# A DeltaNet and Fourier-mix kernel: the block inversion's products as 32x32 blocks, one PE tile each

## Chip, cores and metric

The kernel runs on one core of a Trainium2 chip. The metric is the device time of one execution in microseconds; the profile's span runs from the first to the last instruction of one profiled execution. TensorE (PE in the profile, its weight loads PEld) multiplies matrices, VectorE (DVE), ScalarE (ACT) and GpSimd (POOL) do the elementwise work, SyncE (SP) starts transfers.

## What is computed

Two steps, in float32. First a recurrence per batch and head (4 batches, 8 heads, 768 tokens of 48 values): a 48x48 state is read with the query and then corrected with the key and the value.

```python
k_n = k / (norm(k) + 1e-06)
for t in range(S):
    y[:, :, t] = einsum('bhd,bhde->bhe', q[:, :, t], state)
    v_old = einsum('bhde,bhd->bhe', state, kt)
    state = state + bt * einsum('bhd,bhe->bhde', kt, vt - v_old)
```

The eight heads' outputs lie side by side in a row of 384 values, x. Then, per batch: `mixed = real(fft(fft(x, axis=1), axis=2))`, `u = x + mixed`, a layer norm of u, a two-layer MLP with a ReLU and 1536 hidden values, and u added to its output.

## The kernel before

The tokens of a batch are cut into 6 chunks of 128 (`C`), so there are 24 steps. Three pieces of work belong to a step; each is a Python generator that emits instructions up to its next `yield`.

`pre(n)` (line 232) makes what a chunk needs that doesn't depend on the state. It normalises the keys and scales them with beta, transposes keys and queries on TensorE into `K1T` and `KQT` (lines 256 to 262; two heads of a pair lie in the row halves 0 to 47 and 64 to 111), and forms the Gram products `pg` (lines 269 to 284): for each kind a (keys with keys, keys with queries) and each row half e, four products of 48 rows, one per pair of heads. From them come `Abd` (masked to the diagonal 32x32 blocks), `AT` and `LQ`. Then it inverts the four diagonal 32x32 blocks of I + A of each head, doubling the inverted block from 1 to 32 in five levels (lines 297 to 327). In a level, `px` gets the identity (line 301: a bf16 product with 128x128 weights and 256 columns) and, added to it, A times the inverse so far, T, one product per head; VectorE masks it to `Y` (line 305); `pn` gets the new transposed inverse (half 0, line 315) and, in the three middle levels, the new inverse itself (half 1, line 312); ScalarE copies it to `Tn`. T and its transpose TT are views of `Tn`.

The blocks are kept in two forms. A compact tile has the four 32x32 blocks of a head one below the other on the 128 partitions, 32 columns in all. A wide one, made by `widen` (line 289), has them on the diagonal of 128x128, with zeros elsewhere: it multiplies the compact tile by a mask, five heads on VectorE and three on GpSimd. A product has a wide tile, 128x128, as its weights and a compact one, 32 columns, as what is streamed through them. `Abd` is wide from the start; `Yx` and `TTx` are the widened Y and TT.

`seq(n)` (line 330) is the chunk's step of the recurrence: it solves the triangular system with the inverted blocks, four blocks of 32 tokens in turn (`pu`, 32x32 weights; `pa`, 32 columns of weights), each with a ScalarE copy or a VectorE subtraction between, and then updates the state (`pS`, 128x64 weights, even heads to partitions 0 to 63, odd ones to 64 to 127) and computes the output (`py`).

`post(b)` (line 383) is the second part of a batch: the Fourier products `pf` and `pb`, the layer norm, the MLP's `ph` and `po`.

The loop (lines 477 to 493) advances `seq(n)`, `pre(n+1)` and a share of 13 units (`UNITS`) of a side generator in turn. That is `weights()` in batch 0, which turns the float64 weights into float32 on VectorE and GpSimd, and `post(b-1)` later; the last `post` stands alone at the end. The tile framework places what is emitted in each engine's queue, moving instructions against each other where their data allows it, and adds the semaphore waits.[...] PSUM tiles of `pre` share three buffers (`ps_pre`), those of `seq` two, those of `post` three.

Of the kernel before, what the change touches and what calls it, by code (L numbers as in the profile page):

```python
# [13 lines left out]
ALU = mybir.AluOpType  # L14
ACT = mybir.ActivationFunctionType

C = 128          # tokens of a chunk
W = 32           # width of the diagonal blocks that are inverted explicitly
LEVELS = (1, 2, 4, 8, 16)


def _consts(S, DM):
    """Constants of the shapes: identity, masks and Fourier tables."""
    p = np.arange(128)
    c = np.arange(W)
    r = p % W
    ident = np.eye(128)
    su = (p[None, :] > p[:, None]).astype(np.float64)
    bd = su * (p[None, :] // W == p[:, None] // W)
    grp = (p[:, None] // W == np.arange(128 // W)[None, :]).astype(np.float64)  # L30
    eye_c = (r[:, None] == c[None, :]).astype(np.float64)
    lev = []
    for n in LEVELS:
        off = ((r[:, None] // n) % 2 == 1) & (c[None, :] // n == r[:, None] // n - 1)
        lev.append(eye_c - off)
    pack = np.concatenate([ident, su, bd, grp, eye_c] + lev, axis=1)

    half = S // 2
    s = np.arange(half)

    def seq_table(ks):
        ang = 2.0 * np.pi * (np.outer(s, ks) % S) / S
        t = np.concatenate([np.cos(ang), np.sin(ang)], axis=1)
        return t.reshape(half // 128, 128, -1).transpose(1, 0, 2)

    d = np.arange(DM)
    ang = 2.0 * np.pi * (np.outer(d, d) % DM) / DM
    dt = np.stack([np.cos(ang), -np.sin(ang)])
    dt = dt.reshape(2, DM // 128, 128, DM).transpose(2, 0, 1, 3)

    def f32(a):
        return np.ascontiguousarray(a, dtype=np.float32)

    return dict(pack=f32(pack), even=f32(seq_table(np.arange(0, half + 1, 2))),
                odd=f32(seq_table(np.arange(1, half, 2))), dtab=f32(dt))
# [3 lines left out]
def kernel(  # L59
# [22 lines left out]
    NE = HALF // 2 + 1  # L82
    NO = HALF // 2
    GT = 2
    HV = (5 * H + 7) // 8

    cn = {n: nc.inline_tensor(a, name="k_" + n) for n, a in _consts(S, DM).items()}

# [18 lines left out]
        nc.tensor.matmul(o, lhsT=src, rhs=ident[0:src.shape[0], 0:src.shape[0]],  # L107
                         is_transpose=True, start=start, stop=True, skip_group_check=True)

# [1 line left out]
    NKQ = 2  # L111
    kqs = []
    for i in range(NKQ):
# [43 lines left out]
    nc.scalar.dma_start(out=odt, in_=cn["odd"].ap())  # L157
    nc.scalar.dma_start(out=dtab, in_=cn["dtab"].ap())

    # 0 and 1 are exact in bf16: these only put the identity into an accumulation  # L160
    ident_b = const.tile([128, 128], BF16, name="ident_b")
    nc.vector.tensor_copy(ident_b, ident)
    eye_b = const.tile([128, H, W], BF16, name="eye_b")
# [3 lines left out]
    half_n = const.tile([128, GT], F32, name="half_n")  # L167
    nc.gpsimd.memset(half_n, -0.5)

    # beta with the tokens of a chunk on the partitions  # L170
    psb = ps_pre([128, NC, NBH], "psb")
    for c in range(NC):
        tr(psb[:, c, :], bt[:, c * C:(c + 1) * C], c == 0)
# [1 line left out]
    nc.vector.tensor_copy(bcol.rearrange("p c b h -> p c (b h)"), psb)  # L175

    def weights():
        """The weights come as float64, which no engine computes with: the bits are taken
        apart and each value is rounded to the nearest float32, the widest type there is.
        Float32 weights are loaded as they are."""  # L180
        if moe_w_ch1.dtype == F32:
            nc.sync.dma_start(out=w1, in_=moe_w_ch1.rearrange("(c p) f -> p c f", p=128))
            nc.sync.dma_start(out=w2, in_=moe_w_ch2.rearrange("(c p) m -> p c m", p=128))
# [14 lines left out]
        for i, (_, dst) in enumerate(pieces):  # L198
            w64 = nxt
            if i + 1 < len(pieces):  # L200
                nxt = staged(i + 1)
            lo, hi = w64[:, :, 0], w64[:, :, 1]
            tmp = wk.tile([128, 3, DFF], I32, tag="F", name="wtmp")
            man, exp, low = tmp[:, 0], tmp[:, 1], tmp[:, 2]
            # 1.m from the high word's 20 bits of the mantissa; the low word's added, rounding
            nc.vector.tensor_scalar(man, hi, 3, 0x007FFFF8, op0=ALU.logical_shift_left,
                                    op1=ALU.bitwise_and)
            nc.vector.tensor_scalar(man, man, 0x3F800000, None, op0=ALU.bitwise_or)
            yield
            nc.vector.tensor_scalar(low, lo, 8, None, op0=ALU.logical_shift_right)  # L210
            nc.vector.scalar_tensor_tensor(man.bitcast(F32), low, 2.0 ** -44, man.bitcast(F32),
                                           op0=ALU.mult, op1=ALU.add)
            yield
            # the signed power of two, 0 below float32's range
            nc.vector.tensor_scalar(exp, hi, 20, 0x7FF, op0=ALU.logical_shift_right,
                                    op1=ALU.bitwise_and)
            nc.vector.tensor_scalar(exp, exp, 896, 0, op0=ALU.subtract, op1=ALU.max)
            yield
            nc.vector.tensor_scalar(exp, exp, 255, None, op0=ALU.min)
            nc.vector.tensor_scalar(exp, exp, 23, None, op0=ALU.logical_shift_left)  # L220
            yield
            nc.vector.tensor_scalar(low, hi, 31, 31, op0=ALU.logical_shift_right,
                                    op1=ALU.logical_shift_left)
            nc.vector.tensor_tensor(exp, exp, low, op=ALU.bitwise_or)
            nc.gpsimd.tensor_tensor(dst.rearrange("p c f -> p (c f)"), man.bitcast(F32),
                                    exp.bitcast(F32), op=ALU.mult)
            yield
# [2 lines left out]
    xs = {}  # L230

    def pre(n):
        """What a chunk needs that does not depend on the state."""
        b, c = steps[n]
        kq = kqs[n % NKQ]
        K4, V4 = loaded.pop(n)
# [24 lines left out]
            nc.scalar.activation(dst, pt, ACT.Copy)  # L261
            yield

        # AT[s, h, t] = beta_t k_t.k_s;  LQ[s, h, t] = q_t.k_s for s < t
        AT = wk.tile([128, H, 128], F32, tag="AT", bufs=2, name="AT")
        LQ = wk.tile([128, H, 128], F32, tag="LQ", bufs=2, name="LQ")
        Abd = wk.tile([128, H, 128], F32, tag="Abd", name="Abd")
        hv = "p (j e) t -> p e j t"
        for a in range(2):
            for e in range(2):  # L270
                pg = ps_pre([128, NP, 128], "pg")
                pr = slice(64 * e, 64 * e + D)
                for j in range(NP):
                    mm(pg[:, j, :], K1T[pr, j, :], KQT[pr, a, j, :], j == 0)
                if a == 0:
                    nc.vector.tensor_tensor(Abd.rearrange(hv, e=2)[:, e], pg,
                                            m_bd[:, None, :].broadcast_to([128, NP, 128]),
# [2 lines left out]
                else:  # L280
                    nc.vector.tensor_tensor(LQ.rearrange(hv, e=2)[:, e], pg,
                                            m_su[:, None, :].broadcast_to([128, NP, 128]),
                                            op=ALU.mult)
                yield

        # T = (I + A)^-1 of the diagonal blocks, doubling the block:
        # T2n = Tn Y with Y = I - (A between the halves) Tn. Compact tiles hold
        # only the diagonal blocks; wide ones are block diagonal.
        def widen(src, tag):
            t = wk.tile([128, H, NG, W], F32, tag=tag, name=tag)  # L290
            for eng, hs in ((nc.vector, slice(0, HV)), (nc.gpsimd, slice(HV, H))):
                shape = [128, hs.stop - hs.start, NG, W]
                eng.tensor_tensor(t[:, hs], src[:, hs, None, :].broadcast_to(shape),  # L293
                                  m_grp[:, None, :, None].broadcast_to(shape), op=ALU.mult)
            return t.rearrange("p h g w -> p h (g w)")

        T = TT = TTx = None
        for i in range(len(LEVELS)):
            last = i == len(LEVELS) - 1
            px = ps_pre([128, H, W], "px")  # L300
            mm(px, ident_b, eye_b, True, False)
            for h in range(H):
                mm(px[:, h, :], Abd[:, h, :], eye_c if T is None else T[:, h, :], False, h == H - 1)
            Y = wk.tile([128, H, W], F32, tag="Y", bufs=2, name="Y")
            nc.vector.tensor_tensor(Y, px, m_lev[i][:, None, :].broadcast_to([128, H, W]),  # L305
                                    op=ALU.mult)
            Yx = widen(Y, "Yx")
            yield
            pn = ps_pre([128, 2, H, W], "pn")
            if i > 0 and not last:  # L310
                for h in range(H):
                    mm(pn[:, 1, h, :], TTx[:, h, :], Y[:, h, :], h == 0)
                yield
            for h in range(H):
                mm(pn[:, 0, h, :], Yx[:, h, :], eye_c if TT is None else TT[:, h, :],
                   h == 0 and (i == 0 or last))
            Tn = wk.tile([128, 2, H, W], F32, tag="Tn", bufs=3, name="Tn")
            if i == 0 or last:
                nc.scalar.activation(Tn[:, 0], pn[:, 0], ACT.Copy)
# [2 lines left out]
                nc.scalar.activation(Tn, pn, ACT.Copy)  # L322
                T = Tn[:, 1]
            TT = Tn[:, 0]
            if not last:
                TTx = widen(TT, "TTx")
            yield
        ready[n] = (kq, KQT, AT, LQ, TT, Vb)

    def seq(n):  # L330
        """The chunk's step of the recurrence."""
        b, c = steps[n]
        kq, KQT, AT, LQ, TT, Vb = ready.pop(n)
        st = states[b % 2]
# [46 lines left out]
    out_v = out.rearrange("b (t p) m -> b t p m", p=128)  # L381

    def post(b):
        """Fourier mixing, layer norm and channel MLP of one batch."""
        x = xs.pop(b)
        # cos and sin at s + S/2 are those at s, with the sign (-1)^k
        pm = wk.tile([128, 2, TH, DM], F32, tag="big", bufs=2, name="pm")
        nc.vector.tensor_tensor(pm[:, 0], x[:, 0:TH], x[:, TH:2 * TH], op=ALU.add)
        nc.gpsimd.tensor_tensor(pm[:, 1], x[:, 0:TH], x[:, TH:2 * TH], op=ALU.subtract)
        # F[d, 0, :, k] = sum_s x cos, F[d, 1, :, k] = sum_s x sin  # L390
        F = wk.tile([128, 2, KD, S], F32, tag="F", name="F")
        for dt in range(KD):
            for par, tab, n, hi in ((0, evt, NE, HALF + 1), (1, odt, NO, HALF)):
# [65 lines left out]
                nc.vector.tensor_tensor(x[:, T, :], x[:, T, :], po, op=ALU.add)  # L459
                nc.sync.dma_start(out=out_v[b, T], in_=x[:, T, :])  # L460

    # ---- the chunks of a batch in turn; beside each step, the next chunk's
    # preparation and a share of the previous batch's second part (at first, of the
    # weights' conversion) ----
    UNITS = (2 * KD + 2 * NC + (NC // GT) * (1 + KF + 3 * GT)) // NC + 1

    def advance(gen, n=1):
# [58 lines left out]
```

## Time and profile before

| | before |
|---|---|
| time, median of 2 runs | 1848.38 us (1840.3 and 1856.46) |
| span of the profiled execution | 1847.0 us |
| instructions | 26294 |
| TensorE matmul and weight load busy | 96% and 81% of the span |
| VectorE, ScalarE, GpSimd busy | 31%, 14%, 25% |
| DMA | 32.76 MB, mean 18 GB/s |

A group line of the profile names line, engine and operation, then the tile written and the tiles read (buffer numbers left out), shapes, and the count; behind the bar come the busy time in us and the mean of one in ns, then the time that the engine sat idle before these instructions and what ended it. All matmuls carry line 104, that of the helper `mm`, and transposes line 107, so they are told apart by their tiles. A float32 product appears as two weight loads and two matmuls. Records of neighbouring matmuls overlap, since each is shown from its start to the modelled end of its last result; the distance from start to start is the pace. Slices (part 2) show the busy share in tenths, PEclk the granted share of TensorE's clock.

### The profile page before, as it was taken

What the parts mean: (1) busy time and instruction counts of PE and PEld (TensorE: products, weight loads), DVE (VectorE), ACT (ScalarE), POOL (GpSimd) and SP (SyncE); (2) the same over time, 40 slices, a digit from 0 to 9 for tenths busy, and PEclk for the clock granted to TensorE, in tenths of its full rate; (3) what the DMA queues carried; (4) which work ended last, traced back from release to release, by engine and by line L of the source; (5) the groups of instructions that cost most, each with busy time, mean ns of one, the idle gap of its engine ahead of it and who ended that gap; (6) DMA issues with size and microseconds to landing.
All of it is one profiled execution on the core that took longest, in us unless ns stands there. A gap on an engine that the chain in (4) does not pass through costs nothing. (4 is left out here: it accounts for less than half of the span.)

```text
span 1847.0 us, 26294 instructions
## 1 busy us (share of the span) xinstructions
PE 1773.4 (96%) x11830; PEld 1503.7 (81%) x11830; DVE 578.4 (31%) x919; ACT 253.0 (14%) x505; POOL 453.0 (25%) x356
## 2 busy tenths in 40 slices
PE   4898889989999999999999999999999999999999
PEld 4888889889887897888877897888787888888676
DVE  4534741212123431333232433333323423222211
ACT  1011010101111101101112111111120111111110
POOL 4413422222132230232132231232223212212000
PEclk9999999999997976998798999998999999999999
DMA  7101100000000000000000000000000000000000
GB/s 209 39 9 43 43 5 9 14 5 13 5 1 14 10 9 13 14 14 18 9 9 14 10 9 18 14 22 10 9 10 13 10 10 6 5 6 5 5 9 18
DMA packets 81088, 32.76 MB, mean 18 GB/s; under 512 B 75440, under 2 KB 78512, under 8 KB 80464
## 3 DMA queue, kind: packets, MB, share of 16 engines
q1 hardware_dynamic: 80352, 28.32, 6.1%
q10 hardware_dynamic: 624, 2.76, 0.4%
q8 instruction: 93, 1.52, 0.4%
q14 instruction: 19, 0.16, 0.0%
HBM read 26.35 MB, written 4.72 MB: 17 GB/s over the span
## 5 line engine op out<-in xcount | busy, mean ns | idle before, releaser
L104 PEld LDWEIGHTS pn<-Tn,Yx 128*128 128x128 f32 x1536 | 229.5, 233 | 27.3 <-issue 13.9
L293 POOL TENSOR_TENSOR Yx<-Y,pack 128x384 f32<-128x384 f32 x120 | 166.4, 1386 | 306.4 <-DVE Y L305 286.3
L104 PE MATMUL pn<-Tn,Yx 128*128 128x32 f32 x1536 | 225.7, 307 | 13.8 <-DVE Yx L293 13.8
L104 PE MATMUL ph<-unT,w 128*128 128x256 f32 x864 | 235.5, 414 | 2.0 <-ACT unT L438 2.0
L293 POOL TENSOR_TENSOR TTx<-Tn,pack 128x384 f32<-128x384 f32 x96 | 127.6, 1330 | 372.9 <-ACT Tn L322 314.9
L104 PE MATMUL po<-w,hT 128*128 128x384 f32 x576 | 208.9, 504 | 0.0
L104 PEld LDWEIGHTS px<-Tn,Abd 128*128 128x128 f32 x1152 | 172.8, 235 | 27.2 <-ACT Tn L322 18.4
L104 PEld LDWEIGHTS pn<-Y,TTx 128*128 128x128 f32 x1152 | 168.8, 231 | 22.2 <-DVE Y L305 19.1
L293 DVE TENSOR_TENSOR TTx<-Tn,pack 128x640 f32<-128x640 f32 x96 | 84.6, 881 | 326.4 <-ACT Tn L322 278.3
L104 PE MATMUL px<-Tn,Abd 128*128 128x32 f32 x1152 | 173.5, 311 | 13.3 <-ACT Tn L322 13.3
L104 PEld LDWEIGHTS ph<-unT,w 128*128 128x128 f32 x864 | 164.2, 203 | 25.6 <-ACT unT L438 2.7
L104 PE MATMUL pn<-Y,TTx 128*128 128x32 f32 x1152 | 170.7, 308 | 10.3 <-DVE Y L305 10.3
L104 PEld LDWEIGHTS po<-w,hT 128*128 128x128 f32 x576 | 105.7, 194 | 59.9 <-issue 3.0
L104 PE MATMUL pg<-KQT,K1T 48*128 48x128 f32 x768 | 137.3, 348 | 2.8 <-ACT KQT L261 2.8
L104 PEld LDWEIGHTS pg<-KQT,K1T 48*128 48x128 f32 x768 | 111.6, 236 | 17.2 <-ACT KQT L261 4.4
L293 DVE TENSOR_TENSOR Yx<-Y,pack 128x640 f32<-128x640 f32 x120 | 119.7, 997 | 8.2
L305 DVE TENSOR_TENSOR Y<-px,pack 128x256 f32<-128x256 f32 x120 | 50.7, 423 | 216.6 <-PE px L104 216.5
L104 PE MATMUL pb<-dtab,F 128*128 128x384 f32 x288 | 118.2, 551 | 0.0
L322 ACT ACTIVATE Tn<-pn 128x512 f32<-128x512 f32 x72 | 43.0, 597 | 527.1 <-PE pn L104 527.1
L104 PEld LDWEIGHTS pu<-R,Tn 32*32 32x32 f32 x1280 | 72.4, 123 | 29.6 <-issue 13.2
L248 POOL TENSOR_TENSOR kq<-kq,bcol 128x384 f32<-128x384 f32 x24 | 21.8, 910 | 279.4 <-DVE kq L246 250.3
L352 DVE TENSOR_TENSOR R<-R,pa 32x384 f32<-32x384 f32 x60 | 33.2, 553 | 182.4 <-PE pa L104 182.3
(88 smaller groups left out, 1833.8 us busy)
## 6 DMA issues: line engine op xcount, KB each, us to landing
w<-in_moe_w_ch_dram SPq DMA_DIRECT2D x6, 1536.0 KB, 6.5
K<-in_k_dram SPq DMA_DIRECT2D x24, 192.0 KB, 2.6
V<-in_v_dram SPq DMA_DIRECT2D x24, 192.0 KB, 2.6
kq<-in_q_dram SPq DMA_DIRECT2D x24, 192.0 KB, 2.8
out_dram<-x SPq DMA_DIRECT2D x24, 192.0 KB, 1.9
dtab<-k_dtab ACTq DMA_DIRECT2D x1, 1152.0 KB, 8.3
evt<-k_even ACTq DMA_DIRECT2D x1, 579.0 KB, 5.7
odt<-k_odd ACTq DMA_DIRECT2D x1, 576.0 KB, 6.9
```

The lines of the kernel that those rows point to most:

```text
L104: nc.tensor.matmul(o, lhsT=lhsT, rhs=rhs, start=start, stop=stop, skip_group_check=True)
L248: nc.gpsimd.tensor_tensor(kq[:, 1, :, 0:D], kq[:, 0, :, 0:D], bc[:, :, None].broadcast_to([128, H, D]), op=ALU.mult)
L293: eng.tensor_tensor(t[:, hs], src[:, hs, None, :].broadcast_to(shape), m_grp[:, None, :, None].broadcast_to(shape), op=ALU.mult)
L305: nc.vector.tensor_tensor(Y, px, m_lev[i][:, None, :].broadcast_to([128, H, W]), op=ALU.mult)
L322: nc.scalar.activation(Tn, pn, ACT.Copy)
L352: nc.vector.tensor_tensor(R[rw], R[rw], pa[rw], op=ALU.subtract)
```

## The change

The four diagonal blocks of a head no longer go through one product with 128x128 weights, but through four with 32x32 weights. Block g lies on partitions 32g to 32g+31 of the weights, of the streamed tile and of the output, which is the PE tile of row group g and column group g. So the compact tiles serve as weights too, and the wide ones, `widen` and its mask, fall away. A px or pn block of 8 products becomes one of 32, in the order of heads and, inside a head, of tiles. `pn`'s first write in each 32-partition group starts the accumulation there. In the middle levels half 1 comes before half 0, as before. What is meant: products of different tiles may run beside each other in the array, weights are a quarter as wide, and VectorE and GpSimd lose the widening.

The Gram products now take both PSUM tiles of a kind at once and alternate between the row halves, so that neighbours use different rows of the array; the two masks and copies follow after all eight.

The yields move with it: two instead of four in the Gram part, 18 instead of 13 in the levels. Comments are dropped as well, which moves later lines by one or more.

```diff
@@ pre(n), Gram products
         for a in range(2):
+            pgs = [ps_pre([128, NP, 128], f"pg{e}") for e in range(2)]
+            for j in range(NP):
+                for e in range(2):
+                    pr = slice(64 * e, 64 * e + D)
+                    mm(pgs[e][:, j, :], K1T[pr, j, :], KQT[pr, a, j, :], j == 0)
             for e in range(2):
-                pg = ps_pre([128, NP, 128], "pg")
-                pr = slice(64 * e, 64 * e + D)
-                for j in range(NP):
-                    mm(pg[:, j, :], K1T[pr, j, :], KQT[pr, a, j, :], j == 0)
+                pg = pgs[e]
...
-                yield
+            yield
@@ pre(n), inversion
-        def widen(src, tag):
...
-        T = TT = TTx = None
+        def blocks(o, lhsT, rhs):
+            for h in range(H):
+                for g in range(NG):
+                    rw = slice(W * g, W * g + W)
+                    mm(o[rw, h, :], lhsT(h, g, rw), rhs(h, g, rw), False)
+
+        T = TT = None
...
-            for h in range(H):
-                mm(px[:, h, :], Abd[:, h, :], eye_c if T is None else T[:, h, :], False, h == H - 1)
+            blocks(px, lambda h, g, rw: Abd[rw, h, rw],
+                   (lambda h, g, rw: eye_c[rw]) if T is None else
+                   (lambda h, g, rw: T[rw, h, :]))
...
-            Yx = widen(Y, "Yx")
             yield
             pn = ps_pre([128, 2, H, W], "pn")
-            if i > 0 and not last:
+            first = [True] * NG
+            for a in ((1, 0) if i > 0 and not last else (0,)):
                 for h in range(H):
-                    mm(pn[:, 1, h, :], TTx[:, h, :], Y[:, h, :], h == 0)
+                    for g in range(NG):
+                        rw = slice(W * g, W * g + W)
+                        left, right = (TT, Y) if a else (Y, TT)
+                        r = eye_c[rw] if right is None else right[rw, h, :]
+                        mm(pn[rw, a, h, :], left[rw, h, :], r, first[g])
+                        first[g] = False
                 yield
-            for h in range(H):
-                mm(pn[:, 0, h, :], Yx[:, h, :], eye_c if TT is None else TT[:, h, :],
-                   h == 0 and (i == 0 or last))
...
-            if not last:
-                TTx = widen(TT, "TTx")
             yield
```

## The prediction

> **What bounds the kernel now.** I read the page's busy times first, then its slices, the groups, and the timeline for the pace of single blocks.
>
> ```profile
> PE 1773.4 (96%) x11830; PEld 1503.7 (81%) x11830; DVE 578.4 (31%) x919; ACT 253.0 (14%) x505; POOL 453.0 (25%) x356
> ...
> PEclk9999999999997976998798999998999999999999
> ```
>
> TensorE is busy 96% of the span; no other engine passes a third. The groups tell with what:
>
> ```profile
> L104 PEld LDWEIGHTS pn<-Tn,Yx 128*128 128x128 f32 x1536 | 229.5, 233 | 27.3 <-issue 13.9
> L293 POOL TENSOR_TENSOR Yx<-Y,pack 128x384 f32<-128x384 f32 x120 | 166.4, 1386 | 306.4 <-DVE Y L305 286.3
> L104 PE MATMUL pn<-Tn,Yx 128*128 128x32 f32 x1536 | 225.7, 307 | 13.8 <-DVE Yx L293 13.8
> L104 PE MATMUL px<-Tn,Abd 128*128 128x32 f32 x1152 | 173.5, 311 | 13.3 <-ACT Tn L322 13.3
> L104 PE MATMUL pn<-Y,TTx 128*128 128x32 f32 x1152 | 170.7, 308 | 10.3 <-DVE Y L305 10.3
> ...
> L293 DVE TENSOR_TENSOR Yx<-Y,pack 128x640 f32<-128x640 f32 x120 | 119.7, 997 | 8.2
> ```
>
> With the px and pn groups of the first level these are 742 us of TensorE time: a product loads 128x128 weights to stream 32 columns. Each fp32 product is two passes (1536 records for 768 products), each a weight load and a matmul. A chunk has 13 blocks of eight products, 5 of px and 8 of pn: 208 passes. Means of overlapping records overstate, so I take paces from the timeline (start, length, count):
>
> ```profile
> 468.96 3.62 PE L104 MATMUL px<-Tn,Abd 128*128 128x32 f32 x16 [0.75 <-ACT Tn L322]
> 473.10 3.62 PE L104 MATMUL pn<-Y,TTx 128*128 128x32 f32 x16 [0.52 <-DVE Y L305]
> ```
> ```profile
> 736.18 2.83 PE L104 MATMUL po<-w,hT 128*128 128x384 f32 x8
> 738.84 1.87 PE L104 MATMUL pn<-pack,Yx 128*128 128x32 f32 x16
> 740.54 2.83 PE L104 MATMUL po<-w,hT 128*128 128x384 f32 x8
> ```
> ```profile
> 861.09 0.67 PE L104 MATMUL pS<-U,kq 128*64 128x48 f32 x16
> ```
> ```profile
> 773.91 0.86 PE L104 MATMUL pu<-R,Tn 32*32 32x48 f32 x16
> 774.71 0.76 PE L107 MATMUL pt<-pack,kq 128*128 128x128 f32 x5
> ```
> ```profile
> 776.80 0.38 PE L104 MATMUL ph<-unT,w 128*128 128x256 f32 x1
> 777.11 0.27 PE L104 MATMUL pu<-R,Tn 32*32 32x48 f32 x2
> ```
>
> A block of 16 passes takes 3.4 us from start to start at 470 us and 1.7 to 1.8 at 739 us; single records there are 213 and 112 ns apart. The first is a TensorE at half its clock, although PEclk shows 9 there: the trace's clock records begin at 529 us. So the time has three parts. To 558 us, the first preparation and batch 0's six chunks run at half clock, with little between the blocks. By the first transpose of each preparation in the timeline (86.8, 557.7, 1623.1 us) these six take 78.5 us each. From 558 to about 1690 us, 17 preparations, 66.6 us each, have the previous batch's post work beside them, mostly at full clock. After that comes the end of the post work, which the change doesn't touch. All three are set by TensorE's in-order queue.
>
> **What the Trainium skill says.** "TensorEngine Tiling (Array Packing)", Key Properties: tiles work independently, and a change of tiling mode drains TensorE. The trace agrees: the step from the last ph pass to the first 32x32 pu pass is 309 ns, where ph passes are 216 apart (93 more), and the step back from pu to 128x128 is 131 ns. "TensorE: Matmul & The Clock Gate", section LDWEIGHTS, makes a load's time proportional to its columns: 112 ns per pass with 128 columns; in pS, where two tiles of 64 columns alternate, each tile repeats every 58. Its Part 3 has matmuls of different tiles overlap, with starts 4 ns apart; in pS they start 7 to 8 ns apart, in pairs, and 16 passes start within 0.45 us, so two column tiles of one bank do overlap. Its Part 1 has the clock either at half or full by recent activity; the 213 and 112 ns agree.
>
> **The change, part by part.**
> (1) px and pn: each product becomes four 32x32 products on four tiles, so a block has 64 passes in place of 16. What one tile needs: pu streams 48 columns in 43 ns (40 plus 2.5), so 32 columns take 29; a 32-column load, by 112 and 58, also about 29. Four tiles side by side thus need 29/4 = 7.3 ns per pass, the lower bound: 0.47 us a block. The upper bound is the densest stream the trace has, pS: 58 ns for two passes, 29 each, 1.86 us a block. In pS, bursts of single instructions start 7 to 8 ns apart, and a pair of load and matmul 7 ns after the last, so I expect the queue to hand out a pass every 7 to 15 ns, and take 10: 0.64 us at full clock. At half clock a tile needs 58 ns, four tiles 14.6 per pass; I take 16: 1.0 us.
> Saved per chunk: at full clock 13 x (1.79 - 0.64) = 15.0 us, at half clock 13 x (3.43 - 1.0) = 31.6 us.
> (2) Mode changes, an added cost. px and pn were in the mode of all their neighbours; now some 10 to 11 blocks per chunk go in (+93 ns) and out (131 in place of 29, about +100): 10.5 x 0.19 = 2.0 us at full clock, 4 at half, of which I count 3 since part falls into waits that exist anyway.
> (3) The widening goes: 216 of DVE's instructions and 216 of POOL's (about 204 and 294 us busy). On the path it is only where pn waits for Yx: 1.54 us at 486.1 in the timeline, against 0.52 where pn waits for Y alone. That is about 1 us at each of two levels of a chunk without post work, 1.5 us taken; in later chunks ph, po or pb fill it: nothing.
> (4) Gram products: 32 passes of 112 ns, 3.6 us a chunk. Alternating halves could take half of that; the instruction order shows some still in rows of four, so I take 1.0 us.
> (5) New waits: with short blocks, px to Y to pn (about 0.75 us: 0.2 for the matmul's end, 0.42 for Y, the semaphore) and pn to Tn to px (about 0.9) show where nothing lies between. After 558 us the new order has two or three ph, or four po products between, 0.9 to 2.6 us: covered but for some; 1.5 us per chunk. Before 558 us these waits (0.75 and 0.52 above) are already there. Who waits behind them on TensorE is the whole chunk, since its queue is in order.
>
> Sum: after 558 us 15.0 + 1.0 - 2.0 - 1.5 = 12.5 us x 17 chunks = 212. Batch 0: 31.6 - 3 + 1.5 = 30 x 6 = 180 (Gram left out). First preparation: about 31. 1848 - 212 - 180 - 31 = 1425.
>
> **The rivals.**
> A. Strict order: a product's second pass waits for its tile, and the next tile's first pass comes 7 ns later: 29 + 7 = 36 ns per small product, 1.15 us a block (2.1 at half clock). For it: the program has both passes of a tile together. Against: pS has the same order, and its starts pair from the first to the last record, as if the other tile went ahead. Full clock 13 x 0.64 + 1.0 - 2.0 - 0.5 = 6.8 x 17 = 116; half 13 x 1.33 - 3 + 1 = 15 x 7 = 107: 1625 us.
> B. The instruction stream limits at 29 ns per pass, whatever the clock: 1.86 us a block. For it: nothing denser has been seen, and TensorE's instructions more than double. Against: pS slows with the clock, so its 29 is the load's. Full clock costs 0.9 + 2.0 - 1.0 = 1.9 x 17 = 32, half clock gains 13 x 1.57 - 3 = 17.5 x 7 = 122: 1758 us.
> C. Slower. Tiles with different rows don't overlap, 29 ns a pass and 58 at half clock: 32 lost after 558 us, and (13 x 0.28 + 3) x 7 = 46 before: 1926 us. Or the array, less filled by small tiles, falls to half clock after 558 us too: without the 5 us per chunk that half clock costs now, a chunk is 66.6 - 5 - 12.5 = 49 us; its work but for the blocks and waits (39 us) doubles, so 93 us, 17 x 26 = 449 lost against the 211 gained before: 2086 us. For it: from 667 to 735 us the granted clock was 0.65, in a stretch of px and pn with few post products. Against: the dense post matmuls now fill more of each chunk, not less.
>
> **How the numbers follow.** Forecast 0.70: 7 to 15 ns per pass. At 15 the block is 0.96 us, 13 x 0.83 + 1.0 - 2.0 - 1.0 = 8.8 x 17 = 150, giving 1487; at 7.3, 13 x 1.32 = 17.2 gives 1390, and 1320 to 1340 if the waits vanish and the clock holds throughout (some 80 us are lost now to half clock after 558). A 0.14, B 0.07, C 0.07, other 0.02. The likeliest is 1425. From 1320 to 1640 leaves out B, C and a little below. Faster takes the forecast, A and B (1758 is 5% less): 0.90; within 2% only a mix of B and C: 0.03; slower 0.07.
>
> **What would show it.** Right: px and pn blocks of 64 passes start to end in 0.5 to 1.0 us at full clock, with starts of four tiles in groups; batch 0's chunks near 48 us instead of 78; chunks after that near 54; DVE some 200 and POOL some 290 us less busy; the stretch after the last chunk unchanged, near 155 us. Rival A shows as 1.15 us blocks, B as 1.9 whatever the clock, C as 3.7 us blocks before 558 us or as half clock over the later chunks. The forecast is wrong if TensorE's idle time after 558 us grows beyond a few us per chunk: then the chain through Y and Tn has become the bound.

## The result and the profile after

The changed kernel took 1374.7 us (median of 1373.45 and 1375.95) against 1848.38 us: a ratio of 0.744, with a 95% interval of 0.730 to 0.758. The forecast was 1425 us. A second measurement of it gave the same:

> The changed kernel as it is, on the same chip, to compare the others with: 1365 to 1385 us.

Measured: 1377.1 us, ratio 0.739 (0.735 to 0.744); I use 1377 as its time beside the experiments below. Ratios and medians from here on leave out executions that came out over 1.5% above the fastest of the same kernel.

The page of the kernel after, its busy times, its granted clock and the queue that brings instructions (packets, MB, share):

```profile
PE 1251.3 (91%) x26806; PEld 945.8 (69%) x26806; DVE 370.4 (27%) x703; ACT 251.2 (18%) x505; POOL 156.7 (11%) x140
...
PEclk9985555556999999899999999999999999999999
...
q8 instruction: 210, 3.44, 1.1%
```

TensorE is still the bound, now at 91%. It has 26806 matmuls instead of 11830. VectorE is 208 us less busy and GpSimd 296. The clock records begin at 87 us here, so most of batch 0's half clock is now visible, as the row of fives. The groups that answer to those shown of before:

```profile
L103 PE MATMUL pn<-Tn,Y 32*32 32x32 f32 x6144 | 85.2, 204 | 33.4 <-issue 29.0
L103 PEld LDWEIGHTS pn<-Tn,Y 32*32 32x32 f32 x6144 | 72.6, 116 | 51.4 <-issue 42.7
...
L103 PE MATMUL px<-Tn,Abd 32*32 32x32 f32 x4608 | 65.1, 203 | 34.6 <-issue 26.4
L103 PE MATMUL pg<-KQT,K1T 48*128 48x128 f32 x768 | 88.2, 333 | 2.4 <-ACT KQT L260 2.1
...
L103 PE MATMUL pn<-Y,Tn 32*32 32x32 f32 x4608 | 61.7, 204 | 15.7 <-DVE Y L306 12.0
```

The widening groups are gone. The idle time ahead of px and pn no longer ends with VectorE's Yx; most of it is "issue", time in which TensorE waited for nothing that the profile shows. That column leads to the surprise of this case.

The span in four stretches, each cut at the first transpose of a preparation: the first preparation, batch 0's six chunks, the next 16 chunks, the rest. Columns: window, length, busy time of each engine with its count, granted clock, DMA share, GB/s. Before:

```profile
core 0: us, PE busy (x) PEld busy (x) DVE busy (x) ACT busy (x) POOL busy (x), PEclk, DMA share, GB/s
13.20:86.80 73.60, 55.69 (x258) 52.95 (x258) 42.71 (x50) 5.17 (x9) 31.45 (x20) 1.00 0.29 83
86.80:557.70 470.90, 437.01 (x2506) 406.97 (x2506) 152.82 (x209) 52.08 (x99) 128.33 (x84) 1.00 0.07 18
557.70:1623.10 1065.40, 1061.56 (x7889) 881.21 (x7888) 337.95 (x573) 165.16 (x331) 268.52 (x224) 0.93 0.05 12
1623.10:1847.00 223.90, 218.30 (x1179) 161.84 (x1178) 43.50 (x85) 29.27 (x65) 19.18 (x16) 0.99 0.02 9
```

After:

```profile
13.10:57.00 43.90, 24.71 (x881) 20.41 (x881) 32.62 (x42) 5.16 (x9) 18.41 (x11) 1.00 0.51 143
57.00:345.40 288.40, 253.57 (x6237) 217.38 (x6229) 99.37 (x153) 49.21 (x94) 49.36 (x30) 0.60 0.12 31
345.40:1157.00 811.60, 766.20 (x17881) 561.16 (x17879) 201.09 (x429) 166.40 (x336) 76.99 (x80) 0.99 0.07 17
1157.00:1371.70 214.70, 206.05 (x1817) 146.12 (x1813) 35.82 (x76) 29.17 (x65) 6.59 (x7) 1.00 0.03 10
```

Time without a clock record counts as 1.00 in these windows. There are no records to 529.5 us in the kernel before and to 87.4 us in the kernel after, and both ran at half clock there: a pu block of 16 passes takes 1.48 us at 58 us of the kernel after, and 0.86 at 959 us. With these parts counted as half, batch 0's clock was 0.53 before and 0.55 after.

| stretch | before | after | difference | forecast |
|---|---|---|---|---|
| first preparation | 73.6 | 43.9 | -29.7 | -31 |
| batch 0, six chunks | 470.9 (78.5 each) | 288.4 (48.1 each) | -182.5 | -180 |
| 16 chunks after it | 1065.4 (66.6 each) | 811.6 (50.7 each) | -253.8 | -200 |
| rest, with the 17th preparation | 223.9 | 214.7 | -9.2 | -12.5 |

So the miss of 50 us lies almost wholly in the 16 later chunks. TensorE's busy share there fell from 99.6% to 94%, and yet they gained more than forecast.

The pace of blocks, from the timeline (start, length, operation, count, idle time and what ended it). First a level with post products between its blocks, then one further on in the same chunk:

```profile
1086.67 0.75 PE L103 MATMUL px<-Y,Abd 32*32 32x32 f32 x64
1087.35 2.85 PE L103 MATMUL po<-w,hT 128*128 128x384 f32 x8
1090.13 0.75 PE L103 MATMUL pn<-Y,Tn 32*32 32x32 f32 x64
```

```profile
1103.74 0.72 PE L103 MATMUL pn<-Y,Tn 32*32 32x32 f32 x62
1104.29 0.19 PE L103 MATMUL pn<-Tn,Y 32*32 32x32 f32 x1
1104.29 0.19 PE L103 MATMUL pn<-Y,Tn 32*32 32x32 f32 x1
1104.30 0.19 PE L103 MATMUL pn<-Tn,Y 32*32 32x32 f32 x1
1104.30 0.19 PE L103 MATMUL pn<-Y,Tn 32*32 32x32 f32 x1
1104.32 0.68 PE L103 MATMUL pn<-Tn,Y 32*32 32x32 f32 x58
1106.16 0.25 PE L103 MATMUL pn<-Tn,Y 32*32 32x32 f32 x4 [1.16 <-issue]
```

A block of 64 passes takes 0.75 us from start to end. From its first start to its last it is 0.56 us, 8.9 ns per pass; in batch 0, where the clock is half, it is 0.84 us, 13.4 ns per pass. The second fence shows two things. The block of half 1 (Y,Tn) comes first in the program, then half 0 (Tn,Y); around 1104.29 us products of half 0 start ahead of the last two of half 1. And at its end the last four passes of a block start 1.16 us late, with nothing named that they waited for.

### The profile page after: what moved, and what is told of

Same layout as the page of the kernel before. It is cut to its first block, busy times and chain, and to the rows that moved or that the text cites. A ratio compares the mean times of both kernels' runs of the same rounds, so it can differ in the third digit from the quotient of the medians.

```text
span 1371.7 us, 55579 instructions
## 1 busy us (share of the span) xinstructions
PE 1251.3 (91%) x26806; PEld 945.8 (69%) x26806; DVE 370.4 (27%) x703; ACT 251.2 (18%) x505; POOL 156.7 (11%) x140
## 3 DMA queue, kind: packets, MB, share of 16 engines
q8 instruction: 210, 3.44, 1.1%
## 5 line engine op out<-in xcount | busy, mean ns | idle before, releaser
L306 DVE TENSOR_TENSOR Y<-px,pack 128x256 f32<-128x256 f32 x120 | 50.6, 422 | 251.9 <-PE px L103 251.8
L103 PE MATMUL pn<-Tn,Y 32*32 32x32 f32 x6144 | 85.2, 204 | 33.4 <-issue 29.0
L103 PEld LDWEIGHTS pn<-Tn,Y 32*32 32x32 f32 x6144 | 72.6, 116 | 51.4 <-issue 42.7
L103 PEld LDWEIGHTS px<-Tn,Abd 32*32 32x32 f32 x4608 | 53.6, 114 | 68.4 <-issue 37.3
L103 PE MATMUL px<-Tn,Abd 32*32 32x32 f32 x4608 | 65.1, 203 | 34.6 <-issue 26.4
L103 PEld LDWEIGHTS pa<-U,AT 64*32 64x32 f32 (+2 forms) x1152 | 63.7, 123 | 28.8 <-issue 22.2
L103 PE MATMUL pu<-R,Tn 32*32 32x48 f32 x1280 | 82.1, 222 | 1.2 <-DVE R L353 0.9
L103 PEld LDWEIGHTS pn<-Y,Tn 32*32 32x32 f32 x4608 | 52.3, 115 | 38.6 <-DVE Y L306 19.5
L103 PE MATMUL pn<-Y,Tn 32*32 32x32 f32 x4608 | 61.7, 204 | 15.7 <-DVE Y L306 12.0
L103 PE MATMUL pa<-U,AT 64*32 64x48 f32 (+2 forms) x1152 | 74.4, 225 | 0.0
L103 PEld LDWEIGHTS pb<-dtab,F 128*128 128x128 f32 x288 | 52.0, 191 | 29.6 <-issue 0.6
```

Of the source, the lines that this page charges most:

```text
L103: nc.tensor.matmul(o, lhsT=lhsT, rhs=rhs, start=start, stop=stop, skip_group_check=True)
```

## The experiments

Ratios are to the kernel before, measured on the same chip beside each group, with medians of 1854.9 us for e1, e2, e3 and e5, 1851.1 for e4, e6, e7 and e8, and 1859.2 for e9, e10, e11 and the kernel after again. The theory at the start was the forecast's own: four tiles work beside each other, and the Gram part is a small addition.

**e1, tile by tile.** The same 64 passes, but all eight heads of a tile before the next tile, so that neighbours share a tile.

```diff
 def blocks(o, lhsT, rhs):
-    for h in range(H):
-        for g in range(NG):
+    for g in range(NG):
+        for h in range(H):
```

(The loop of pn is turned in the same way.)

> The changed kernel with the 32 products of a block in the order of tiles (all heads of tile 0, then of tile 1 and so on) in place of heads; same products, same count. Theory (the gain is the overlap of the four tiles): neighbours now share a tile, so a pass takes 27 to 29 ns at full clock and about 53 at half, a block 1.7 to 1.9 us and 3.4 us; batch 0's chunks go from 48 back to 75 to 80 us, the later ones to 62 to 66, the time to 1780 to 1880 us; the pauses inside blocks (72 us in the changed kernel) vanish, since instructions are used more slowly. If the clock follows how much of the array is filled, its mean falls below that of the changed kernel (0.908) and chunks after batch 0 get longer still. Rival (narrow weights and the missing widening bring the gain): within 3% of 1375 us.

Measured: 2022.5 us, ratio 1.090 (1.077 to 1.102). Blocks in the timeline, at full clock and in a stretch at half clock, and the window of the 16 later chunks:

```profile
1284.84 3.06 PE L103 MATMUL px<-Tn,Abd 32*32 32x32 f32 x64
...
1315.29 1.91 PE L103 MATMUL px<-pack,Abd 32*32 32x32 f32 x64
```

```profile
500.80:1773.70 1272.90, 1272.02 (x17880) 1000.59 (x17879) 201.87 (x429) 167.87 (x336) 76.82 (x80) 0.74 0.05 11
```

With the same instructions, the same widths and the widening gone all the same, the order of two loops is worth 645 us. Within one tile, passes follow each other by 31 to 32 ns at full clock and 53 to 54 at half. Where one tile gives way to the next their products overlap, so the mean of a whole block is 27 and 45 ns per pass. A block that takes 0.75 us on four tiles in turn takes 1.91 on one tile after the other, no better than the 1.87 of before. So most of the gain is the overlap of tiles. What is left for the rest shows in the first five chunks of batch 0, which ran at half clock in before and e1 and nearly so (0.53) in the kernel after: 80.5 us each before, 70.5 in e1, 48.5 after. Of these 32 us the order of the products makes 22. The other 10 go to the narrower weights, the missing widening, the Gram part and e1's own overlaps between tiles. The time is above the 1780 to 1880 that a steady clock would have given, since the later chunks ran at a granted clock of 0.74 (79.6 us each), though TensorE was busy without a break. Busy time alone does not hold the clock up.

**e2, the change without its Gram part, and e3, the Gram part alone on the kernel before.** Both are the same lines, taken back in e2 and put in in e3:

```diff
 for a in range(2):
+    pgs = [ps_pre([128, NP, 128], f"pg{e}") for e in range(2)]
+    for j in range(NP):
+        for e in range(2):
+            ...
+            mm(pgs[e][:, j, :], K1T[pr, j, :], KQT[pr, a, j, :], j == 0)
     for e in range(2):
-        pg = ps_pre([128, NP, 128], "pg")
-        for j in range(NP):
-            mm(pg[:, j, :], K1T[pr, j, :], KQT[pr, a, j, :], j == 0)
+        pg = pgs[e]
```

> The changed kernel with the Gram part undone (four products of one row half, then four of the other, two yields more). Theory (row halves overlap in the changed kernel): pg goes back from 84 to about 130 us from start to start, the time to 1405 to 1420 us. Rival (the alternation does nothing, pg is shorter because the clock is up): 1370 to 1385 us, with pg passes near 56 ns in pairs in both.

> The kernel before with the Gram alternation alone. Theory: 32 passes a chunk go from 112 to some 60 ns, at half clock from 213 to some 110, less what the neighbours' waits take back: 24 chunks x 1.7 to 2.3 us, 1795 to 1810 us. Rival (hidden or lost to the later masks, since both PSUM tiles now finish together): 1840 to 1850 us.

Measured: e2 1441.0 us, ratio 0.775 (0.766 to 0.784); e3 1788.5 us, ratio 0.966 (0.955 to 0.976). The Gram part is worth 64 us on top of the blocks (1441.0 - 1377.1) and 66 us alone (1854.9 - 1788.5), more than either expectation had. The group of pg in before, in e2 and in e3:

```profile
L104 PE MATMUL pg<-KQT,K1T 48*128 48x128 f32 x768 | 137.3, 348 | 2.8 <-ACT KQT L261 2.8
```

```profile
L103 PE MATMUL pg<-KQT,K1T 48*128 48x128 f32 x768 | 132.4, 338 | 2.2 <-ACT KQT L260 2.1
```

```profile
L104 PE MATMUL pg<-KQT,K1T 48*128 48x128 f32 x768 | 94.7, 342 | 3.1 <-ACT KQT L261 2.7 <-ACT AT L281 0.4
```

The alternation takes 40 us off the products themselves (the distances from start to start add up to 130 us in before, 125 in e2, 84 in the kernel after, 90 in e3). The rest goes with a better clock: 0.97 in the later chunks of e3 against 0.93 in before, 0.99 in the kernel after against 0.97 in e2. In e3 nearly all of the gain lies there: 61.7 us per later chunk against 66.6, but 78.1 against 78.5 in batch 0. Of the 79 us that these 16 chunks gained, the clock makes some 45 (an estimate: 1065 x 0.07 against 987 x 0.03). The forecast had 1.0 us per later chunk, 17 us in all.

**e4, no widening in the kernel before.** The same 128x128 weights for all products, but always the same wide tile, made once, so that nothing has to be widened. Half 0 of pn streams Y, so that it still waits for Y, and the inverse is not computed.

```diff
 def widen(src, tag):
-    t = wk.tile([128, H, NG, W], F32, tag=tag, name=tag)
...
+    return wide_fixed
```

> The kernel before without the widening: the wide weights are one fixed tile, and half 0 of pn streams Y, so that it still waits for Y; the computation of the inverse is left out in that sense. Theory (the widening lies beside TensorE's work and shows only where pn waits for Yx in the chunks without post work): some 1 to 2 us in each of the first seven preparations, 1830 to 1845 us beside a kernel before of 1850. Rival (the relief of DVE and POOL, 204 and 294 us, was a large part of the gain): 60 us or more below the kernel before.

Measured: 2081.2 us, ratio 1.123 (1.111 to 1.136): slower by 230 us where both theories had a gain or nothing. The later chunks went from 66.6 to 79.4 us at a clock of 0.77. Batch 0's six chunks took 78.9 against 78.5 us each, and the first preparation 68.1 against 73.6. One guess was the data: the fixed tile is mostly zeros. The other was the order: with no widening in the way, the framework puts fewer post products between the blocks.

**e9, the same with a filled tile.** The four diagonal blocks hold values of the cosine table times 0.2.

```diff
-nc.vector.memset(wide_fixed, 0.0)
-nc.vector.tensor_copy(wide_fixed[:, :, 0:W], eye_c[...])
+nc.vector.tensor_scalar(filled_s, filled, 0.2, None, op0=ALU.mult)
+nc.vector.tensor_tensor(wide_fixed[...], filled_s[...], m_grp[...], op=ALU.mult)
```

> As the kernel before without the widening (one fixed wide tile as weights, half 0 of pn streams Y, the inverse not computed), but the fixed tile is filled like a real one: block-diagonal, its blocks full of cosines times 0.2, where the earlier run had the identity in one column block and zeros. Theory (the earlier run fell to half clock since most of its operands were zero; the widening itself is worth little): the mean clock returns to 0.94 to 0.97 and the time to 1825 to 1850 us beside a kernel before of 1850 to 1865. Rival (the clock falls whenever the widening is gone, by the order of the work): clock near 0.85 and 2000 us or more again.

Measured: 2070.7 us, ratio 1.112 (1.103 to 1.121), later chunks 79.3 us at 0.77. The data is not the reason. The timeline of a late level of e9:

```profile
1322.78 1.49 PE L104 MATMUL po<-w,hT 128*128 128x384 f32 x2
1324.06 3.46 PE L104 MATMUL px<-Tn,Abd 128*128 128x32 f32 x16
1327.33 1.63 PE L104 MATMUL po<-w,hT 128*128 128x384 f32 x2
```

Here one po product (two passes) stands between blocks, where before had four (eight passes, at 736 and 740 us in the prediction's fence), and the block takes 3.46 us, its length at half clock. So the clock again goes with the mix of work: long stretches of narrow products with little dense work between them. That the order of the queue is the cause of the fall fits what was seen; e4 and e9 change the order only as a side effect, so it was not isolated. What they do price is the widening at equal clock. Batch 0 as a whole hides it: its sixth chunk ran in part at full clock in before (a px block takes 1.87 us at 552 us) and at half in e4. The first five chunks ran at half clock in all three. Their windows in before, e4 and e9:

```profile
86.80:489.50 402.70, 368.81 (x2079) 348.52 (x2079) 137.27 (x187) 39.63 (x75) 111.41 (x74) 1.00 0.08 21
```

```profile
81.40:474.20 392.80, 372.27 (x2078) 348.43 (x2079) 95.21 (x144) 39.45 (x75) 47.80 (x29) 1.00 0.08 21
```

```profile
83.20:475.10 391.90, 371.38 (x2078) 347.93 (x2079) 94.43 (x143) 39.57 (x75) 47.83 (x29) 1.00 0.08 21
```

That is 80.5, 78.6 and 78.4 us per chunk. The widening is thus worth some 2 us per chunk there, if the changed order has no part in it, and 4 to 5.5 us once in the first preparation.

**e5, the identity in tile mode.** px's first product, the bf16 identity, is the only 128x128 product inside the inversion itself. As four products of 32x32 it leaves the tiling mode unchanged up to the block.

```diff
-mm(px, ident_b, eye_b, True, False)
+for g in range(NG):
+    rw = slice(W * g, W * g + W)
+    mm(px[rw], ident_b[rw, rw], eye_b[rw], True, False)
```

> The changed kernel with the identity of px also put in by four 32x32 products, so that px needs no change of the array's mode in its middle. Theory (a mode change costs some 90 ns each way): 5 levels x 0.2 us x 24 chunks, twice that in the first 7 preparations: 25 to 35 us less, 1340 to 1350 us. Rival (the six more instructions per level cost as much in TensorE's supply of instructions, or the mode changes lie in waits): 1370 to 1385 us.

Measured: 1378.4 us, ratio 0.742 (0.736 to 0.748), chunks of 48.3 and 50.8 us: no difference from 1377. Changes of mode, as far as this edit removes them, cost nothing that can be seen in the end.

**The pauses.** The "issue" time of the groups led to a list of all pauses inside px and pn blocks: places where more than 0.3 us lie between the starts of two neighbouring passes, with no wait on the instruction behind. The kernel after has 62, 71.7 us together, the longest 4.7 us. Counted over all of TensorE's records (26806 weight loads, 26806 matmuls, 92 semaphore and drain instructions), every one of the 62 lies at the same place: behind the 192nd of each 256 records. 53704 such records and the 210 packets of the instruction queue make 256 to a packet (3.44 MB / 210 = 16 KB each). At each pause the next matmul starts 1.2 to 1.6 us after the end of the packet that landed last, and 2.2 to 3.0 us after that packet's start. Where packet after packet has a pause, the restarts are mostly 3.4 to 4.0 us apart, which is 13 to 16 ns per record. The kernel before had 93 packets for 23756 records, no pause over 0.65 us inside a block and none bound to that place. The reading is that TensorE's instructions arrive 256 at a time, and that a block which uses them up every 4.5 ns (a load and a matmul per 8.9 ns) outruns the supply. e1 agrees: with the same 210 packets, but an instruction every 14 ns at full clock (27 ns per pass), it has no pause. Three experiments test the reading further.

**e6, the post work spread.** A chunk's 13 units of post work come in the first rounds of the loop; here they are spread over 25 rounds, so that more of the blocks have dense products between them.

```diff
+    turn += 1
-    if share:
+    if share and (not live or turn * UNITS // 25 > UNITS - share):
         share -= 1
```

> The changed kernel with the 13 units of side work of a chunk spread evenly over its 25 rounds in place of its first 13. Theory (pauses inside px and pn blocks come from TensorE running out of instructions where blocks follow each other with little between): with post work between all levels the pauses, 72 us in the changed kernel, fall below 30 us and the time to 1330 to 1350 us. Rival (the pauses don't depend on what lies between, or the early levels now show the waits that the late ones lose): 1365 to 1385 us.

Measured: 1377.9 us, ratio 0.743 (0.732 to 0.754). The pauses fell from 72 to 51 us, the time did not. The later chunks' clock was 0.97 instead of 0.99, worth about 16 of the 21 us (an estimate: 811 x 0.02); whether that is all is open.

**e8, half the instructions for the same columns.** Each product streams the 64 columns of two heads through the even head's weights, in px and pn alike; the odd heads' own weights are left out.

```diff
-for h in range(H):
+for h in range(0, H, 2):
     for g in range(NG):
-        mm(o[rw, h, :], lhsT(h, g, rw), rhs(h, g, rw), False)
+        mm(o[rw, h:h + 2, :], lhsT(h, g, rw), rhs(h, g, rw), False)
```

> The changed kernel with px and pn products that stream 64 columns, two heads, through the weights of the even head; half of the products (and of their instructions) are left out, the odd heads get the even heads' weights. At half clock the array's time of a block stays (32 passes of 26.7 ns in place of 64 of 13.3), at full clock it goes from 0.57 to about 0.43 us. Theory (the pauses come from the supply of instructions): pauses below 15 us in place of 72, batch 0's chunks 1 to 2 us shorter although their blocks take as long, 1270 to 1300 us. Rival (the pauses are the array's or PSUM's): pauses of 60 us and more remain, 1335 to 1350 us.

Measured: 1250.6 us, ratio 0.675 (0.667 to 0.682), with 132 packets, and not one pause. The gain of 126 us is more than the 72 us of pauses and more than was expected: a block fell from 0.56 to 0.44 us from its first start to its last (13 x 0.127 us x 18 preparations outside batch 0's stretch = 30 us), and batch 0's chunks from 48.1 to 42.1 us at a clock of 0.64 instead of 0.55 (the profile has 0.70 and 0.60, since it counts some 30 us without records as full). So e8 shows that the pauses go with the number of instructions, and at most 72 of its 126 us are theirs.

**e7, dense products as filler in batch 0.** Four bf16 products of 128x128 weights and 256 columns per round of the loop, which nobody reads.

```diff
     live = [g for g in live if advance(g)]
+    if b == 0:
+        pd = ps_post([128, 2 * H, W], "pd")
+        for i in range(4):
+            mm(pd[:, 0:H, :], ident_b, eye_b, True)
```

> The changed kernel with dense products that nobody reads (bf16, 128x128 weights, 256 columns, four per round of the loop) in batch 0, which has no post work. Theory (TensorE's clock follows how much of the array works; batch 0 is at half clock since its products are small): the clock is full in most of batch 0, its chunks go from 48 us to 38 to 44 us although about 100 products of 0.11 us are added, and the time to 1300 to 1345 us. Rival (the clock stays at half, or the filler costs what it brings): chunks of 60 us and more, 1440 us or more; in between, 1360 to 1390, if both cancel.

Measured: 1353.9 us, ratio 0.729 (0.723 to 0.735). The window of batch 0's chunks:

```profile
57.20:317.60 260.40, 231.40 (x6706) 189.70 (x6696) 97.58 (x153) 48.24 (x93) 49.76 (x30) 0.90 0.13 32
```

With some 470 more products (6706 matmuls against 6237) the chunks became shorter, 43.4 us instead of 48.1, as the granted clock rose from 0.55 to 0.90 (here the records begin at 9 us). The time is 23 us below the kernel after, which ran on another chip, and misses the 1300 to 1345 us expected; e11 against e10, on one chip, gives 20 us. The pauses grew to 85 us: the faster array outruns the supply more often.

**e10, transposes on VectorE.** If instructions are the limit, fewer of them should pay. The transposed inverse of the first four levels comes from a 32x32 block transpose on VectorE, and pn keeps one half: 9 blocks per chunk instead of 13.

```diff
-for a in ((1, 0) if i > 0 and not last else (0,)):
...
+if i == 0:
+    T = Y
+else:
+    left, right = (Y, TT1) if last else (TT1, Y)
...
+            mm(pn[rw, h, :], left[rw, h, :], right[rw, h, :], h == 0)
+    nc.scalar.activation(T, pn, ACT.Copy)
+if last:
+    TT = T
+else:
+    nc.vector.transpose(TT.rearrange("p h w -> p (h w)"), T.rearrange("p h w -> p (h w)"))
```

> The changed kernel with the transposed inverse made by VectorE's transpose of 32x32 blocks in place of products: pn's half 0 goes in the first four levels, so 9 blocks of 32 products per chunk are left of 13; all is computed. Theory (after the change TensorE is short of instructions, 256 of which go with each block pair): array time 4 x 0.57 = 2.3 us per chunk at full clock and 3.4 at half, most of the pauses, and a wait less in level 0: some 5 us x 17 + 6 us x 7, 1240 to 1270 us, pauses below 25 us. Rival (the transposes lengthen the chain between px and pn): 1340 us or more.

**e11, e10 with e7's filler.**

> The same with the unread dense products of the filler run in batch 0 as well. Theory (clock and instruction supply are two separate costs): another 20 to 30 us less than the run with the transposes alone, 1215 to 1250 us. Rival (with shorter chunks the filler is itself on the path): the same or more than without it.

Measured: e10 1242.2 us, ratio 0.667 (0.663 to 0.672); e11 1222.6 us, ratio 0.657 (0.653 to 0.661), 155 us below the kernel after. In e10 the transposes' groups, the window of the 16 later chunks, and the instruction queue:

```profile
L326 DVE STREAM_TRANSPOSE TTn<-Tn 128x256 f32<-128x256 f32 x72 | 31.3, 435 | 68.5 <-ACT Tn L321 68.4
...
L326 DVE STREAM_TRANSPOSE TTn<-Y 128x256 f32<-128x256 f32 x24 | 10.7, 444 | 0.6
```

```profile
313.70:1032.40 718.70, 711.01 (x13802) 519.98 (x13799) 228.73 (x493) 151.94 (x321) 76.99 (x80) 1.00 0.08 18
```

```profile
q8 instruction: 161, 2.64, 0.9%
```

96 transposes of 0.44 us on an engine that is two thirds idle take the place of 6144 small passes. TensorE is 99% busy in the later chunks, at full clock, and the pauses are down to 9.9 us. Of e10's gain of 135 us, four blocks fewer account for 4 x 0.56 x 18 = 40 us beyond batch 0 and 4 x 0.84 x 6 = 20 in it, the pauses for 62 (an estimate); 13 us are left over for waits, changes of mode and the clock.

| | time, us | batch 0 chunk | later chunk | pauses: count, us |
|---|---|---|---|---|
| before | 1848 to 1859 | 78.5 | 66.6 | see text |
| after | 1377 | 48.1 | 50.7 | 62, 71.7 |
| e1 tile by tile | 2022.5 | 71.1 | 79.6 | 0 |
| e2 no Gram part | 1441.0 | 50.3 | 54.2 | 72, 82.4 |
| e5 identity in tiles | 1378.4 | 48.3 | 50.8 | 63, 77.2 |
| e6 post spread | 1377.9 | 48.4 | 50.7 | 48, 50.8 |
| e7 filler | 1353.9 | 43.4 | 50.6 | 65, 84.5 |
| e8 half the instructions | 1250.6 | 42.1 | 45.7 | 0 |
| e10 transposes | 1242.2 | 44.1 | 44.9 | 14, 9.9 |
| e11 both | 1222.6 | 40.7 | 45.1 | 24, 19.1 |

## Why the prediction was right, and what it sized wrongly

The mechanism was the one forecast, and the two stretches at half clock came out within 3 us of it. In batch 0 that is partly luck. The blocks gave 1.9 us per chunk more than was taken, and the Gram products, left out there, 0.6 (e3) to 2.4 us (e2); pauses that had no term in the forecast took 2.6 back (15 us in six chunks). Nor did all of batch 0 run at half clock, as the prediction has it: before, clock records from 529.5 us on show its last 28 us mostly at full. The later chunks gained 254 us instead of 200. By the prediction's own steps:

**(1) Blocks.** Taken at 10 ns per pass and 0.64 us at full clock, 16 ns and 1.0 us at half. Measured 8.9 ns (0.57 us) and 13.4 ns (0.85 us). Saved per chunk at full clock: 13 x (1.79 - 0.57) = 15.9 us instead of 15.0. At half clock 13 x (3.43 - 0.85) = 33.5 instead of 31.6. e1 shows the cause, and with it the limit: each tile works at its own pace. Call four passes, one on each tile, a round. At half clock a round takes one tile's repeat (4 x 13.4 = 54 ns, and e1 has 53 to 54). At full clock e1 has 31 to 32 ns, where the prediction took 29 for one tile; the blocks at 1086.67 and 1101.07 us have rounds of 32 ns in their first half and of about 33 in the last third. Longer rounds at the start and between (52, 37 and about 49 ns) raise the mean to 36 (4 x 8.9); what they are is open.

**Rival A** asked for 36 ns per small product and 1.15 us a block, because each tile would wait for its own second pass. The blocks are half that, and the timeline at 1104.29 us shows why: a product of one tile starts ahead of an earlier one of another. The Trainium skill, "TensorE: Matmul & The Clock Gate", Part 3, has matmuls start and end strictly in program order; the starts in this trace contradict it for four tiles on the array's diagonal, by a few passes. **Rival B**, 29 ns per pass whatever the clock, had the right resource and the wrong place: within a block a pass starts every 8.9 ns, but the supply in packets of 256 is a limit that shows as pauses.

**(2) Changes of mode.** Taken at 2.0 us per chunk from the 309 and 131 ns steps of before. e5 removed one kind of change per block pair and gained nothing, so this price is not confirmed as a cost on the path; the changes at the ends of blocks were not tested.

**(3) The widening.** Taken at 1.5 us per chunk in batch 0. At equal clock e4 and e9 show about 2 us (78.6 and 78.4 against 80.5), so this term held; the first preparation had 4 to 5.5 us. VectorE's 208 and GpSimd's 296 us came as forecast, and all but this was off the path. What the widening was worth in the later chunks can't be told, as the clock fell in both experiments.

**(4) The Gram products.** Undersized. Taken at 1.0 us per chunk after 558 us and left out before; measured 1.9 us per chunk from the products' starts alone, 64 to 66 us in all by e2 and e3, much of it with the clock. The prediction kept back half of it because the instruction order showed some still in rows of four.

**(5) New waits.** Taken at 1.5 us per later chunk and put down to the chain through Y and Tn. From the sum: blocks 15.9, Gram 1.9 and the clock 4.1 (below) make 21.9, the chunk gained 15.9, so 6.0 us per chunk went to waits and changes of mode, where (2) and (5) together had 3.5. TensorE's idle time there grew from 4 to 45 us, 2.6 per chunk, and the pauses of instruction supply inside blocks make 2.9 from start to start (47 us in these 16 chunks), so the idle time is in the main theirs and not that of Y and Tn. The other 3.4 are no idle time: changes of mode, for which (2) had 2.0, or an error of this sum. The prediction saw that instructions more than double, but held this against a pace per instruction only, in rival B.

**The clock.** By this reckoning it is what made most of the miss: the sum kept the later chunks' clock as it was. Before, it was 0.93 there: 1065 x 0.07 = 75 us lost. After, 0.99: 8 us. (Both are estimates that let all work in the stretch go with the clock.) The difference, 66 us or 4.1 per chunk, is more than the 54 us by which the stretch beat its forecast. The prediction had named these 80 us only as the lower end of the range. The fall of the clock in rival C is a real danger, as e1, e4 and e9 show (0.74 to 0.77); here the change went the other way. That fits the blocks' smaller share of a chunk and the dense post products' larger one, and e7 shows the effect of dense products by itself, in batch 0; for the later chunks no run isolates it.

**What stays open:** what the longer rounds in a block at full clock are; which measure of activity decides the clock; the widening's worth in later chunks; whether the clock is all that kept e6 from gaining, though a third of the pauses went.

## What to carry to other kernels

Products of small blocks belong on different tiles of the array, in an order in which neighbours use different tiles: the same instructions ordered the other way were 645 us slower. Then count TensorE's instructions, since cutting a product into four multiplies them, and their supply in packets of 256 can become the next limit; a product that another, idle engine can replace (here a transpose) is worth more than its array time. And read the granted clock stretch by stretch before pricing anything, with an eye on where its records begin: an edit that changes the share of dense work between narrow products can move the clock, and with it the price of all the rest. Compare a single term only over stretches at the same clock; the widening's 2 us per chunk can't be seen otherwise.

## What the runs showed of the hardware

- TensorE's instructions arrive in 16 KB packets, one to 256 records. Blocks of small products that use one every 4.5 ns stood 62 times for 0.3 to 4.7 us, always behind the 192nd of 256 records. Half the instructions for the same columns had no pause (e8), nor had the same instructions at one every 14 ns (e1).
- Four tiles on the array's diagonal, in turn, start a 32x32 fp32 pass every 8.9 ns at full clock and 13.4 at half. On one tile it takes 31 to 32 ns and 53 to 54 (e1). Matmuls of different tiles can start ahead of each other by a few passes (1104.29 us).
- A TensorE that is busy without a break can still fall to a mean granted clock of 0.74 (e1) or 0.77 (e9) when its work is narrow; some 470 unread dense products raised a stretch from 0.55 to 0.90 and shortened it by 28 us (e7).
- The clock records can begin late: the kernel before is shown at 1.00 to 529.5 us, where its passes of 128 columns of weights start 213 ns apart, against 112 at full clock.
- A 128x256 fp32 transpose in 32x32 blocks takes VectorE 0.44 us (e10).
